# Seven half-size products for gate and value in the last two blocks of an attention and GEGLU kernel, over a fixed turn of PSUM banks

## The chip, the cores and the metric

The kernel runs on one core of one Trainium2 chip. The metric is the device time of one execution in microseconds (us). Each batch of runs was taken on one chip together with fresh runs of the kernel before; its medians were 344.80, 344.44 and 344.56 us in the three batches.

Engines in the profile: PE is TensorE, DVE is VectorE, ACT is ScalarE, POOL is GpSimd. In a timeline the columns are start (us), duration (us), engine, source line, operation, output<-inputs, shapes, count, and in brackets the idle time before it with its releaser. Matmul ends are modelled, so starts are what counts. The same statement has other line numbers in each kernel (the multiply that makes hid is L325 before and L340 after).

## The reference, cut to what matters

```python
# attention without softmax, 8 batches x 8 heads x 576 tokens x 64
kv  = einsum('bhsd,bhse->bhde', k, v)
out = einsum('bhsd,bhde->bhse', q, kv)
x   = out / rms(out) * g_norm                  # 4608 tokens x 512 after a transpose
# GEGLU and a gated residual
hid = gelu(x @ w_gate) * (x @ w_val)           # 512 -> 1536, twice
y   = x + sigmoid(x @ w_res) * (hid @ w_out)   # 1536 -> 512
```

The tokens are cut into nine blocks of 512. Block 8 holds what is left of the eight batches (64 tokens of each); a batch's part of it is called the remainder. While TensorE multiplies block b, the other engines prepare the attention of the next batch.

## The kernel before: the parts that matter

Gate and value of a block are twelve slots, each with four matmuls of 512 columns for gate and four for value. Each slot takes two PSUM banks (the buffers that matmuls write to, eight in all) from a rotating pool of four. The bank of gate comes free when ScalarE has made Gelu of it, the bank of value when VectorE has made `hid`. In the traces `t` is the attention output after its norm, `osb` the output tile, and `ws` and `ts` are the change's sums of weights and of tokens.

```python
pmoe  = ctx.enter_context(tc.tile_pool(name="pmoe",  bufs=4, space=bass.MemoryType.PSUM))
pattn = ctx.enter_context(tc.tile_pool(name="pattn", bufs=4, space=bass.MemoryType.PSUM))

def m_gval(blk, f, pool=pmoe, tag="mm"):
    ...
    gps = pool.tile([P, NJ * P], FP32, tag=tag, name="gps")
    m_mm(gps, wg_c, f, blk, 0, NJ)
    vps = pool.tile([P, NJ * P], FP32, tag=tag, name="vps")
    m_mm(vps, wv_c, f, blk, 0, NJ)
    m_act(blk, f, gps, vps)        # ge = Gelu(gps) on ScalarE, hid = ge * vps on VectorE

def m_res(blk, j, pool=pmoe, tag="mm"):
    rps = pool.tile([P, C], FP32, tag=tag, name="rps")
    ...                            # four matmuls of 512 columns, then Tanh on ScalarE
```

Behind the slots come four residual tiles (`m_res`), then the output product, which is already made of seven products of half size (Strassen's scheme in Winograd's form):

```python
def res(jj):
    for j in (2 * jj, 2 * jj + 1):
        m_res(blk, j)
    if jj == 1:
        pmoe.tile([P, C], FP32, tag="mm", name="none")   # keeps the turn even
...
prod(w["E"], a_of(blk, 1, 2), b_of(2, 1), False)
pf((0, 0), w["E"])                                 # VectorE
prod(w["A"], s_[2], wo_t[:, 2], False)
sub(nc.vector, c22, w["A"], w["d"], ALU.add)       # frees w["A"] for the last product
prod(w["F"], s_[3], b_of(2, 2), False)
...
prod(w["A"], a_of(blk, 2, 2), wo_t[:, 3], False)   # the last product
```

## Time and profile before

| | kernel before |
|---|---|
| time, median of three runs | 344.58 us (344.43 to 345.43) |
| span of the profiled run | 345.4 us |
| TensorE busy | 331.9 us, 96% |
| VectorE busy | 236.5 us, 68% |
| GpSimd busy | 103.1 us, 30% |

The span is the time between the first and the last record on the core. The device time is about 2 us longer than the span of the same run.

The waits of TensorE, costliest first (in us: total, how often, longest), show that it waits for nearly nothing behind the opening:

```profile
PE kvp L718 <- DVE v L689: 2.5, 2, 2.3
PE wA L431 <- DVE wF L404: 1.2, 1, 1.2
PE idle L668 <- DVE zeros L641: 1.2, 1, 1.2
PE vps L783 <- DVE t L757: 0.6, 1, 0.6
PE vps L336 <- DVE hid L325: 0.4, 1, 0.4
```

Only the second of these (in block 1, at 91.35 us) and the last (in block 2, at 117.72) lie outside the opening.

### The profile page before, as it was taken

The page shows a single profiled execution, that of the slowest core. Times are in us where ns is not written, and L with a number is a line of the kernel's source. Part 1 is how long each engine was busy: PE and PEld are TensorE (multiplying, and loading weights), DVE is VectorE, ACT ScalarE, POOL GpSimd, SP SyncE. Part 2 cuts the span into 40 slices and gives each one's busy share as a digit, 9 for nine tenths or more (in the row PEclk, how much of TensorE's full clock was granted, in tenths as well). Part 3 has the DMA queues.
Part 4 walks back from the last instruction along what each step waited for, and adds up shares of the span by engine and source line. Part 5 has one row for each costly group of instructions (what it writes and reads, how often), then busy time and mean ns, then how long its engine had stood idle before and what let it go on. Part 6 is the DMA issues. An engine that isn't in the chain of part 4 may idle for free.

```text
span 345.4 us, 6165 instructions
## 1 busy us (share of the span) xinstructions
PE 331.9 (96%) x2432; PEld 188.0 (54%) x2432; DVE 236.5 (68%) x446; ACT 150.1 (43%) x265; POOL 103.1 (30%) x121
## 2 busy tenths in 40 slices
PE   8789999999899999999999999999999999999992
PEld 3544454445744475447544764476447644764481
DVE  5665549769859987698578976885688735453643
ACT  3573384274336352535263615361736133623350
POOL 2692161980064108200820083005000600050013
PEclk9899999999999999999999999999999999999997
DMA  7999999669589263966395439744003120030004
GB/s 244 290 178 204 195 204 166 168 95 150 117 108 164 94 123 120 165 60 128 130 167 43 102 114 174 79 92 153 17 0 61 63 76 2 1 121 4 0 2 121
DMA packets 76399, 38.81 MB, mean 112 GB/s; under 512 B 42066, under 2 KB 73810, under 8 KB 76370
## 3 DMA queue, kind: packets, MB, share of 16 engines
q0 software_dynamic: 38752, 17.17, 40.1%
q1 hardware_dynamic: 37184, 20.71, 21.6%
q10 hardware_dynamic: 434, 0.52, 0.5%
q8 instruction: 19, 0.31, 0.4%
q14 instruction: 10, 0.08, 0.1%
HBM read 38.80 MB, written 9.44 MB: 140 GB/s over the span
## 4 chain that ended last, share of the span: by engine, by line
PE 69%; DVE 2%; issue 0%; POOL 0%; POOLq 0%; DVEq 0%
PE gps L336 21%; PE vps L336 20%; PE wA L431 10%; PE rps L356 6%; PE wF L431 3%; PE wD L431 2%; PE w L431 2%; PE wE L431 2%; PE kvp L187 1%; PE op L205 1%; DVE t L282 1%; DVE hid L325 1%; DVE hid_s L404 0%; DVE t L296 0%; POOL osb L526 0%
## 5 line engine op out<-in xcount | busy, mean ns | idle before, releaser
L324 ACT ACTIVATE ge<-gps 128x512 f16<-128x512 f32 x108 | 64.3, 597 | 133.1 <-PE gps L336 127.8
L325 DVE TENSOR_TENSOR hid<-ge,vps 128x512 f16<-128x512 f16 x108 | 73.8, 684 | 63.2 <-PE vps L336 60.8
L336 PE MATMUL vps<-xT,wv 128*128 128x512 f16 x424 | 108.8, 379 | 0.4 <-DVE hid L325 0.4
L336 PE MATMUL gps<-xT,wg 128*128 128x512 f16 x424 | 109.0, 379 | 0.0
L470 POOL TENSOR_TENSOR osb<-osb,t 128x512 f32<-128x512 f32 x28 | 36.1, 1309 | 155.6 <-DVE osb L466 148.6
L336 PEld LDWEIGHTS <-wv 128*128 128x128 f16 x424 | 41.5, 98 | 50.6 <-issue 0.7
L336 PEld LDWEIGHTS <-wg 128*128 128x128 f16 x424 | 40.2, 98 | 45.4 <-issue 0.4
L431 PEld LDWEIGHTS <-hid_s 128*128 128x128 f16 x384 | 37.5, 98 | 6.3 <-issue 1.4
L356 PE MATMUL rps<-wr,xT 128*128 128x512 f16 x144 | 32.7, 379 | 0.0
L431 PEld LDWEIGHTS <-hid 128*128 128x128 f16 x288 | 28.2, 98 | 5.1
L365 ACT ACTIVATE th<-rps 128x512 f32<-128x512 f32 x36 | 21.5, 597 | 19.0 <-PE rps L356 19.0
L356 PEld LDWEIGHTS <-xT 128*128 128x128 f16 x144 | 14.1, 98 | 16.8
L224 DVE TENSOR_REDUCE ss<-sq 128x8 f32<-128x512 f32 x32 | 20.6, 679 | 2.9 <-ACT sq L222 2.7
L431 PE MATMUL wA<-wo_ts,hid_s 128*128 128x256 f16 x168 | 20.6, 273 | 1.2 <-DVE wF L404 1.2
L370 ACT ACTIVATE th<-th 128x512 f32<-128x512 f32 x36 | 19.9, 622 | 0.0
L282 DVE TENSOR_TENSOR t<-op,ny 128x512 f16<-128x512 f32 x28 | 17.9, 682 | 0.1
L222 ACT ACTIVATE sq<-op 128x512 f32<-128x512 f32 x28 | 15.3, 597 | 4.5 <-PE op L205 4.2
L296 DVE TENSOR_TENSOR t<-t,g 128x512 f16<-128x512 f16 x36 | 16.2, 498 | 0.1
L404 DVE TENSOR_TENSOR hid_s<-hid 128x1536 f16<-128x1536 f16 x16 | 15.3, 955 | 0.3
L526 POOL TENSOR_TENSOR osb<-osb,t 128x512 f32<-128x512 f32 (+1 forms) x4 | 4.3, 1078 | 27.8 <-DVE osb L522 27.8
L373 PE MATMUL fps<-wo,hid 128*128 128x512 f16 x48 | 11.2, 379 | 0.0
L431 PE MATMUL wD<-wo_ts,hid_s 128*128 128x256 f16 x84 | 10.3, 273 | 0.1
(133 smaller groups left out, 326.5 us busy)
## 6 DMA issues: line engine op xcount, KB each, us to landing
out_dram<-osb SPq DMA_DIRECT2D x14, 512.0 KB, 2.6
qraw<-in_q_dram POOLq DMA_DIRECT2D x7, 512.0 KB, 8.2
kraw<-in_k_dram POOLq DMA_DIRECT2D x7, 512.0 KB, 9.9
v<-in_v_dram POOLq DMA_DIRECT2D x7, 512.0 KB, 11.9
out_dram<-osb SPq DMA_DIRECT2D x5, 256.0 KB, 2.8
wg<-in_moe_w_gate_dram POOLq DMA_DIRECT2D x2, 512.0 KB, 9.2
wv<-in_moe_w_val_dram POOLq DMA_DIRECT2D x2, 512.0 KB, 9.4
wo<-in_moe_w_out_dram POOLq DMA_DIRECT2D x2, 512.0 KB, 14.2
```

The costliest lines, as they stand in the source:

```text
L222: nc.scalar.activation(out=sq, in_=src, func=AF.Square)
L224: nc.vector.tensor_reduce(out=out_, in_=sq, op=ALU.add, axis=mybir.AxisListType.X)
L282: nc.vector.tensor_tensor(out=t, in0=o, in1=scale, op=ALU.mult)
L296: nc.vector.tensor_tensor(out=t_t[blk][:, jj, :], in0=t_t[blk][:, jj, :], in1=g16, op=ALU.mult)
L324: nc.scalar.activation(out=ge, in_=gps, func=AF.Gelu)
L325: nc.vector.tensor_tensor(out=hids[blk][:, f, :], in0=ge, in1=vps, op=ALU.mult)
L336: nc.tensor.matmul(ps[:, j0 * P : j1 * P], lhsT=w[:, cc, :], rhs=xT_t[blk][:, j0:j1, cc, :], start=(cc == 0 and j0 == 0), stop=(cc == NP - ...
L356: nc.tensor.matmul(rps, lhsT=xT_t[blk][:, j, cc, :], rhs=wr16[:, cc, :], start=(cc == 0), stop=(cc == NP - 1),)
L365: nc.scalar.activation(out=th, in_=rps, func=AF.Tanh, scale=0.5)
L370: nc.scalar.activation(out=th, in_=th, func=AF.Copy, scale=0.5, bias=0.5)
L431: nc.tensor.matmul(ps[:, e - es[0], :], lhsT=a[:, f, e * P : (e + 1) * P], rhs=b[:, f, :], start=(start and e == es[0] and f == 0), stop=( ...
L470: nc.gpsimd.tensor_tensor(out=res_all[of], in0=res_all[of], in1=t_t[blk][of], op=ALU.add)
```

## The change

It takes matmul time from TensorE. In blocks 7 and 8, gate and value are computed in three groups of seven half-size products instead of eight. For that, sums of quarters of the weights and of the tokens must be made by VectorE and GpSimd. The weight sums are made in block 6, in buffers that attention no longer needs. The groups use all eight PSUM banks, so the two rotating pools become one pool with a fixed tag a bank, and a small class gives out the banks in a fixed turn, in every block.

```diff
-    pmoe = ctx.enter_context(tc.tile_pool(name="pmoe", bufs=4, space=bass.MemoryType.PSUM))
-    pattn = ctx.enter_context(tc.tile_pool(name="pattn", bufs=4, space=bass.MemoryType.PSUM))
+    psum = ctx.enter_context(tc.tile_pool(name="psum", bufs=1, space=bass.MemoryType.PSUM))
+    class Banks:
+        ...
+        def tile(self, shape, dtype, name, tag=None, bank=None):
+            if bank is None:
+                n = self.n - len(self.opening)
+                bank = self.turn[n % 4] if n >= 0 else self.opening[n]
+                self.n += 1
+            self.last = bank
+            return psum.tile(shape, dtype, tag=f"bank{bank}", name=name)
+    pmoe, pattn = Banks((3, 2, 1, 0), (0, 1, 2)), Banks((4, 5, 6, 7))
 ...
-    moep = ctx.enter_context(tc.tile_pool(name="moep", bufs=3))
+    moep = ctx.enter_context(tc.tile_pool(name="moep", bufs=5))
 ...                                      # the sums of tokens of block 7, inside block 6's output products
             pf((0, 0), w["E"])
+            for f in rest:
+                f()
             prod(w["A"], s_[2], wo_t[:, 2], False)
 ...                                      # a group: digits are products, E a copy, d a copy, F and c sums, g Gelu, h hidden values
+        for word in """1g 1v Eg 5g Ev 5v dg 6g dv 6v Fg 2g Fv 2v 7g g11 7v cg 3g cv 3v h11 g22 4g g12 h12 * 4v g21 h22 h21""".split():
 ...                                      # banks of block 6's residuals, and the sums
+    out_at = {LAST[0] - 1: {j: 4 + j for j in range(NJ)}}
+            if blk == LAST[0]:
+                for j, f in enumerate(token_sums(B, nc.gpsimd, "kraw")):
+                    plan.setdefault(j * 2, []).append(f)
+            if blk == LAST[0] - 1:
+                units = [(n, g) for g in range(NF // GF) for n in "gv"]
+                todo = [f for u in units[:4] for f in weight_sums(u, nc.gpsimd)]
+                for j, f in enumerate(todo):
+                    plan.setdefault(2 + j // 2, []).append(f)
+                todo = [f for u in units[4:] for f in weight_sums(u, nc.vector)]
+                for j, f in enumerate(todo):
+                    plan.setdefault(3 + j // 2, []).append(f)
+                rest = token_sums(LAST[0], nc.vector, "qraw")
```

More of the change, by code (lines that the diff above doesn't have):

```diff
@@ L55, with __init__ @@
     hidp = ctx.enter_context(tc.tile_pool(name="hidp", bufs=1))
-    moep = ctx.enter_context(tc.tile_pool(name="moep", bufs=3))
+    moep = ctx.enter_context(tc.tile_pool(name="moep", bufs=5))
     finp = ctx.enter_context(tc.tile_pool(name="finp", bufs=2))
-    pmoe = ctx.enter_context(tc.tile_pool(name="pmoe", bufs=4, space=bass.MemoryType.PSUM))
-    pattn = ctx.enter_context(tc.tile_pool(name="pattn", bufs=4, space=bass.MemoryType.PSUM))
+    psum = ctx.enter_context(tc.tile_pool(name="psum", bufs=1, space=bass.MemoryType.PSUM))
+    class Banks:
+        def __init__(self, turn, opening=()):
+            self.turn, self.opening, self.n, self.last = turn, opening, 0, None
+        def tile(self, shape, dtype, name, tag=None, bank=None):
[6 more added lines that the diff above has]
+    pmoe, pattn = Banks((3, 2, 1, 0), (0, 1, 2)), Banks((4, 5, 6, 7))
     ctx.enter_context(tc.manual_schedule())
@@ L351, in m_gval, with m_res @@
         m_act(blk, f, gps, vps)
-    def m_res(blk, j, pool=pmoe, tag="mm"):
-        rps = pool.tile([P, C], FP32, tag=tag, name="rps")
+    def m_res(blk, j, bank=None):
+        rps = pmoe.tile([P, C], FP32, name="rps", bank=bank)
         for cc in range(NP):
@@ L438, in prod, with out_by_products @@
                 )
-    def out_by_products(blk, later):
+    out_banks = {}
+    def out_by_products(blk, later, banks=None, rest=()):
         w = {}
         s_ = hid_sums
+        banks = banks or {}
         def res(jj):
             for j in (2 * jj, 2 * jj + 1):
-                m_res(blk, j)
-            if jj == 1:
-                pmoe.tile([P, C], FP32, tag="mm", name="none")
+                m_res(blk, j, banks.get(j))
+            if jj == 1 and 3 not in banks:
+                pmoe.n += 1
         def first_two():
             for n in ("D", "E", "F", "A"):
-                w[n] = pmoe.tile([P, 2, CH], FP32, tag="mm", name="w" + n)
+                w[n] = pmoe.tile([P, 2, CH], FP32, name="w" + n, bank=banks.get(n))
+                out_banks[n] = pmoe.last
             w["d"] = finp.tile([P, 2, CH], FP32, tag="wd", bufs=1, name="wd")
@@ L508, in out_by_products, with out_last, bank @@
         return [lambda: res(0), lambda: res(1), first_two, others]
-    def out_last(blk):
+    def out_last(blk, banks):
         s_ = hid_sums
-        def bank(n, pool, tag):
-            return pool.tile([P, n, CH], FP32, tag=tag, name="w")
+        def bank(n, i):
+            return pmoe.tile([P, n, CH], FP32, name="w", bank=i)
         def part(j, n, ch):
@@ L533, in run @@
         def run():
-            wa = [bank(1, pattn, "at") for _ in range(2)]
-            wd, we, wf = [bank(2, pmoe, "mm") for _ in range(3)]
+            wa = [bank(1, banks["A"][e]) for e in range(2)]
+            wd, we, wf = [bank(2, banks[n]) for n in "DEF"]
             d = finp.tile([P, 2, CH], FP32, tag="wd", bufs=1, name="wd")
@@ L549, in run @@
             plus(0, 2, 0, nc.gpsimd)
-            m_res(blk, 3)
+            m_res(blk, 3, banks[3])
             m_sigmoid(3)
@@ L567, in run, with pairs_of @@
             store(2, 2, 0, CH)
-        return [lambda: [m_res(blk, j) for j in range(3)], run]
+        return [lambda: [m_res(blk, j, banks[j]) for j in range(3)], run]
+    LAST = (B - 1, B)
+    GF = 4
+    gv_sums, x_sums = {}, {}
+    def pairs_of(ws, f0):
+        i, o = 0, f0 * P
+        while o >= WCS[i]:
+            i, o = i + 1, o - WCS[i]
+        n = min(WCS[i] - o, GF * P)
+        parts = [ws[i][:, :, o : o + n]]
+        if n < GF * P:
+            parts.append(ws[i + 1][:, :, 0 : GF * P - n])
+        return [p.rearrange("p c (r i f) -> p r i c f", i=2, f=P) for p in parts]
@@ new lines, in w_quadrant, with weight_sums, one @@
+    def w_quadrant(ws, f0, i, k):
+        return [p[:, :, i, 2 * k : 2 * k + 2, :] for p in pairs_of(ws, f0)]
+    def weight_sums(unit, eng):
+        n, g = unit
+        ws = wg_c if n == "g" else wv_c
+        def one(s_, x, y, op):
+            if s_ == 0:
+                tag = ("q16", "k16", "v16")[len(gv_sums) // 2]
+                gv_sums[unit] = qkvp.tile([P, 4, 2, 2, P], FP16, tag=tag, name="ws")
+            sums = gv_sums[unit]
+            of = {t: w_quadrant(ws, GF * g, *t) for t in (x, y) if not isinstance(t, int)}
+            parts = len(w_quadrant(ws, GF * g, 0, 0))
+            for e in range(parts):
+                rs = slice(e * 2 // parts, (e + 1) * 2 // parts)
+                x_, y_ = (sums[:, t, rs] if isinstance(t, int) else of[t][e] for t in (x, y))
+                sub(eng, sums[:, s_, rs], x_, y_, op)
+        return [
+            lambda: one(0, (1, 0), (1, 1), ALU.add),
+            lambda: one(1, 0, (0, 0), ALU.subtract),
+            lambda: one(2, (0, 0), (1, 0), ALU.subtract),
+            lambda: one(3, (0, 1), 1, ALU.subtract),
+        ]
@@ new lines, in x_quadrant, with token_sums, one @@
+    def x_quadrant(blk, k, j):
+        return xT_t[blk][:, 2 * j : 2 * j + 2, 2 * k : 2 * k + 2, :]
+    def token_sums(blk, eng, tag):
+        def one(i, x, y):
+            if i == 0:
+                x_sums[blk] = stage.tile([P, 4, 2, 2, P], FP16, tag=tag, name="ts")
+            t = x_sums[blk]
+            x_, y_ = (t[:, n] if isinstance(n, int) else x_quadrant(blk, *n) for n in (x, y))
+            sub(eng, t[:, i], x_, y_)
+        return [
+            lambda: one(0, (0, 1), (0, 0)),
+            lambda: one(1, (1, 1), 0),
+            lambda: one(2, (1, 1), (0, 1)),
+            lambda: one(3, (1, 0), 1),
+        ]
@@ new lines, in gv_group, with tile_of, product, seed @@
+    def gv_group(blk, g, banks, amid=()):
+        if g == 0:
+            hids[blk] = hidp.tile([P, NF, NJ * P], FP16, tag="hid", name="hid")
+        f0 = GF * g
+        ps, ge, sb = {}, {}, {}
+        def tile_of(n, u):
+            ps[n, u] = pmoe.tile([P, 2, PR], FP32, name=n + u, bank=banks[u, n])
+            return ps[n, u]
+        def product(p, u):
+            ws = wg_c if u == "g" else wv_c
+            n = {1: "A", 2: "E", 3: "F", 4: "A", 5: "F", 6: "A", 7: "A"}[p]
+            first = p in (1, 5)
+            out_ = tile_of(n, u) if first else ps[n, u]
+            s_of = {3: 3, 5: 0, 6: 1, 7: 2}
+            t_of = {4: 3, 5: 0, 6: 1, 7: 2}
+            quad = {1: (0, 0), 2: (0, 1), 4: (1, 1)}
+            xq = {1: (0, 0), 2: (1, 0), 3: (1, 1)}
+            for r in range(2):
+                for c in range(2):
+                    if p in s_of:
+                        lhsT = gv_sums[u, g][:, s_of[p], r, c, :]
+                    else:
+                        i, k = quad[p]
+                        parts = w_quadrant(ws, f0, i, k)
+                        lhsT = parts[0][:, r, c, :] if len(parts) == 1 else parts[r][:, 0, c, :]
+                    rhs = x_sums[blk][:, t_of[p], :, c, :] if p in t_of else x_quadrant(blk, *xq[p])[:, :, c, :]
+                    nc.tensor.matmul(
+                        out_[:, r, :],
+                        lhsT=lhsT,
+                        rhs=rhs,
+                        start=(first and r == 0 and c == 0),
+                        stop=(c == 1),
+                        skip_group_check=True,
+                    )
+        def seed(u):
+            nc.scalar.copy(out=tile_of("E", u), in_=ps["A", u])
+        def keep(u):
+            sb["d", u] = attnp.tile([P, 2, PR], FP32, tag="sq", name="d")
+            nc.scalar.copy(out=sb["d", u], in_=ps["F", u])
+        def plus(u, n):
+            if n == "F":
+                dst = tile_of("F", u)
+            else:
+                dst = sb["c", u] = attnp.tile([P, 2, PR], FP32, tag="o32", name="c")
+            nc.vector.tensor_tensor(out=dst, in0=ps["A", u], in1=sb["d", u], op=ALU.add)
+        quarter = {"11": ("E", 0, 0), "12": ("F", 0, 1), "21": ("A", 1, 0), "22": ("c", 1, 1)}
+        def source(q, u):
+            n = quarter[q][0]
+            return sb[n, u] if n == "c" else ps[n, u]
+        def gelu(q):
+            ge[q] = moep.tile([P, 2, PR], FP16, tag="ge", name="ge")
+            nc.scalar.activation(out=ge[q], in_=source(q, "g"), func=AF.Gelu)
+        def hidden(q):
+            _, i, j = quarter[q]
+            dst = hids[blk][:, f0 + i : f0 + GF : 2, j * PR : (j + 1) * PR]
+            eng = nc.gpsimd if q == "22" else nc.vector
+            eng.tensor_tensor(out=dst, in0=ge[q], in1=source(q, "v"), op=ALU.mult)
+        for word in """1g 1v Eg 5g Ev 5v dg 6g dv 6v Fg 2g Fv 2v 7g g11 7v cg 3g cv 3v h11 g22 4g g12 h12 * 4v g21 h22 h21""".split():
+            if word == "*":
+                for f in amid:
+                    f()
+            elif word[0].isdigit():
+                product(int(word[0]), word[1])
+            elif word[0] == "E":
+                seed(word[1])
+            elif word[0] == "d":
+                keep(word[1])
+            elif word[0] in "Fc":
+                plus(word[1], word[0])
+            elif word[0] == "g":
+                gelu(word[1:])
+            else:
+                hidden(word[1:])
@@ L932, in plan_attn, with banks_of @@
             at(m, NF + 3, lambda: a_x(b, NJ), lambda: d_xT(b, NJ, NJ + 1))
+    out_at = {LAST[0] - 1: {j: 4 + j for j in range(NJ)}}
+    def banks_of(blk):
+        if blk == LAST[0]:
+            w = out_banks
+            first = {"g": (w["D"], w["F"], w["E"], w["A"]), "v": (4, 5, 6, 7)}
+        else:
+            w = out_at[LAST[0]]
+            first = {"g": (w[0], w[2], w["D"], w["A"]), "v": (w[1], w[3], w["E"], w["F"])}
+        groups = []
+        for g in range(NF // GF):
+            groups.append({})
+            for u, (a0, e, f, a1) in first.items():
+                if g % 2:
+                    a0, e, f = a1, f, e
+                groups[g].update({(u, "A"): a0, (u, "E"): e, (u, "F"): f})
+        (ga0, ge_, gf, ga1), (va0, ve, vf, va1) = first["g"], first["v"]
+        out_at[blk] = {0: ga1, 1: va1, 2: ge_, 3: ve}
+        if blk == LAST[0]:
+            out_at[blk].update(A=gf, D=vf, E=ga0, F=va0)
+        else:
+            out_at[blk].update(A=(gf, vf), D=ga0, E=va0, F=ga1)
+        return groups
     late = []
@@ L947 @@
             slots = [lambda f=f: m_gval(blk, f) for f in range(NF)]
+            sevens = blk in LAST
+            if sevens:
+                slots = [None] * NF
+                ends = banks_of(blk)
+                mid = [lambda: s_begin(blk)]
+                for g in range(NF // GF):
+                    slots[GF * g] = lambda g=g: gv_group(blk, g, ends[g], mid if g == 2 else ())
             if blk == 1:
@@ L952, with products @@
             slots += [lambda i=i: outs[i]() for i in range(4 if blk < B else 2)]
-            plan.setdefault(NFH + 2, []).insert(0, lambda: s_begin(blk))
-            def products(blk=blk, outs=outs):
+            if not sevens:
+                plan.setdefault(NFH + 2, []).insert(0, lambda: s_begin(blk))
+            if blk == LAST[0]:
+                for j, f in enumerate(token_sums(B, nc.gpsimd, "kraw")):
+                    plan.setdefault(j * 2, []).append(f)
+            rest = ()
+            if blk == LAST[0] - 1:
[7 more added lines that the diff above has]
+                rest = token_sums(LAST[0], nc.vector, "qraw")
+            def products(blk=blk, outs=outs, rest=rest):
                 s_rest(blk)
-                outs.extend(out_by_products(blk, blk == 1) if blk < B else out_last(blk))
+                outs.extend(
+                    out_by_products(blk, blk == 1, out_at.get(blk), rest) if blk < B else out_last(blk, out_at[blk])
+                )
             plan.setdefault(NF - 1, []).append(products)
```

## The prediction

> **What bounds the kernel now.** I read four views in this order: the page, the timeline of TensorE in blocks 6 to 8, the timelines of VectorE and GpSimd over the same stretch, and the waits of TensorE.
>
> The page first:
>
> ```profile
> PE 331.9 (96%) x2432; PEld 188.0 (54%) x2432; DVE 236.5 (68%) x446; ACT 150.1 (43%) x265; POOL 103.1 (30%) x121
> PE   8789999999899999999999999999999999999992
> PE gps L336 21%; PE vps L336 20%; PE wA L431 10%; PE rps L356 6%; PE wF L431 3%; PE wD L431 2%; PE w L431 2%; PE wE L431 2%; PE kvp L187 1%; PE op L205 1%; DVE t L282 1%; DVE hid L325 1%; DVE hid_s L404 0%; DVE t L296 0%; POOL osb L526 0%
> ```
>
> TensorE is busy in 96% of the span, in nines in nearly every slice, and the chain that ended last is TensorE work. In such a kernel matmul time that is taken away shortens the run one for one, and any new wait of TensorE lengthens it one for one. The timeline of TensorE in block 7 shows how tight it is:
>
> ```profile
> 271.75 1.03 PE L336 MATMUL gps<-xT,wg 128*128 128x512 f16 x4
> 272.62 1.03 PE L336 MATMUL vps<-xT,wv 128*128 128x512 f16 x4
> ...
> 292.47 3.62 PE L356 MATMUL rps<-wr,xT 128*128 128x512 f16 x16
> 295.93 1.47 PE L431 MATMUL wA<-wo,hid 128*128 128x256 f16 x12
> 297.24 1.47 PE L431 MATMUL wD<-wo_ts,hid_s 128*128 128x256 f16 x12
> ```
>
> Columns: start, duration with its modelled end, instruction. Starts are what counts. Gate and value of block 7 run from 271.75 to 292.47, 20.72 us for 96 matmuls of 512 columns, so 215.9 ns each. Twelve matmuls of 256 columns take 297.24 - 295.93 = 1.31 us, so 109.2 ns each. Nothing idles between.
>
> VectorE is the second engine to watch, in block 6 above all:
>
> ```profile
> 250.77 0.69 DVE L325 TENSOR_TENSOR hid<-ge,vps 128x512 f16<-128x512 f16 x1 [0.39 <-PE vps L336]
> 252.50 0.69 DVE L325 TENSOR_TENSOR hid<-ge,vps 128x512 f16<-128x512 f16 x1 [1.04 <-PE vps L336]
> ...
> 260.58 1.42 DVE L296 TENSOR_TENSOR t<-t,g 128x512 f16<-128x512 f16 x4
> ...
> 262.63 0.96 DVE L404 TENSOR_TENSOR hid_s<-hid 128x1536 f16<-128x1536 f16 x1
> ```
>
> After the idle 1.04 us at 252.50 VectorE has no idle time until 265. Its first sum of hidden values (262.63, done 263.6) serves the product wD at 263.89: only 0.3 us of slack at the end of block 6. Blocks 7 and 8, which have no attention beside them, leave VectorE idle 1.04 us of every 1.73.
>
> Last, what VectorE and GpSimd do to each other, from their timelines at 61 and at 273 us:
>
> ```profile
> 61.26 1.66 DVE L107 COPY q<-qraw 128x2048 f16<-128x2048 f16 x1
> 62.33 5.38 POOL L404 TENSOR_TENSOR wo_ts<-wo,wo_ts 128x512 f16<-128x512 f16 x4
> 63.44 1.04 DVE L107 COPY k<-kraw 128x2048 f16<-128x2048 f16 x1
> ...
> 271.41 4.40 POOL L470 TENSOR_TENSOR osb<-osb,t 128x512 f32<-128x512 f32 x3 [1.29 <-DVE osb L466]
> 273.54 1.26 DVE L296 TENSOR_TENSOR t<-t,g 128x512 f16<-128x512 f16 x1
> ```
>
> The multiply t<-t,g takes 0.42 us alone (four in 1.42 us at 260.58, so 0.34 apart) but 1.26 us at 273.54, beside GpSimd. The four wo_ts operations at 62.33 take 5.38 us, where GpSimd needs 1.13 us each undisturbed (three in 3.38 us at 66.56).
>
> **What the Trainium skill says.** (1) "TensorE: Matmul & The Clock Gate", section "Back-to-back issue gap": 262 cycles for 256 columns, 109.2 ns at 2.4 GHz. The trace agrees (109.2 ns). (2) "SBUF — State Buffer", section "SBUF: two separate sides": the port pair that VectorE and GpSimd share is an exclusive lock; a GpSimd operation, or a VectorE operation with two SBUF inputs or in a two-port mode, holds it for the whole instruction and the other blocks. The trace agrees: 0.42 becomes 1.26 us, while hid (one of its inputs in PSUM) stays at 0.67 to 0.69 us beside GpSimd. (3) "GPSIMD Engine Reference", section "Elementwise — side-by-side cycle accounting": about 2.6 cycles an element with two inputs. At 1.2 GHz that is 1.11 us for 512 elements, as in the trace, so I estimate 0.62 us for 256 (half, and some overhead); no row shows that form without a VectorE conflict.
>
> **The change, part by part.**
>
> Removed: 96 matmuls of 512 columns in each of blocks 7 and 8, 20.72 us a block. Added: 3 groups x 7 products x 2 (gate, value) x 4 matmuls of 256 columns = 168, at 109.2 ns 18.35 us. Gain 2.38 us a block, 4.76 us in all, if TensorE never waits. That is 1.4% of 344.6, so even a perfect change does not reach 2%.
>
> Waits inside a group. A group is 14 slots of 0.437 us, 6.12 us. ScalarE has 4 copies and 4 Gelus, 4.7 us at 0.57 to 0.60; VectorE 4 sums and 3 products, at most 4.8 us at 0.69 (0.60 apart). Both fit. Following the order: the sum Fg can start 2.46 us into the group (after product 6 and ScalarE's copy d) and ends at 3.15; product 7 of gate, which needs it, has its slot at 3.50. Fv ends at 3.75, its slot is at 3.93; the sums c end at 4.90 and 5.50, their slots are at 5.24 and 5.68. Slack is 0.1 to 0.3 us everywhere, so I count no wait in the steady state. At the end of a block the third group's last hid ends some 2.1 us after the group, the first sum at 3.1, the second at 4.1; residual (3.45 us, 2.6 in block 8) and the first product (1.31) cover both. In the first group of block 7 VectorE is late with the remainder's t and its multiply (they end 3.05 us after the block's start in the trace before): 0.3 us.
>
> Added to block 6, VectorE: eight sums of weights (512 elements, 16 bit, two SBUF inputs; like t<-t,g, 0.42 us) in pairs in slots 3 to 6. GpSimd: 16 sums of 256 and 8 of 512, 16 x 0.62 + 8 x 1.12 = 18.9 us from 239.9 (when the last output sum of block 5 ends) to about 259, exactly where VectorE's pairs fall.
> I walked VectorE's queue by hand with the rows' durations. A value bank comes free when hid is done, and TensorE needs it two slots later.
> - Without conflict: pairs of 0.8 us. The idle time after slot 3 (1.9 us) takes most of 3.2 us; TensorE waits 0.9 us.
> - With the lock, each sum after the first waits for a GpSimd operation, and GpSimd for it: about 1.3 us a sum. Pair 1 ends at 248.3, pair 2 at 252.7, hid of slot 5 at 253.4 (249.8 before); the value matmuls of slot 7 start 253.5, not 251.36: 2.1 us. Pair 3 ends at 256.4, hid 6 at 257.1: 4.05 in all. Pair 4 ends 258.9, hid 7 at 259.6: 4.9. The norm (2.4 us and a last wait) and hid 8, 263.0: 6.5 us.
>
> Residual banks of block 6: they are now those of attention, and the order by engine shows the first residual waiting for the third t, which VectorE reaches behind hid of slot 10: 1.3 us more, in both cases.
>
> Token sums of block 7: four sums on VectorE between pf(0,0) (268.79) and the sum c22, which the last product waits for at 270.44. They take 1.6 us, so c22 ends at 271.1: 0.7 us. But GpSimd's first output sum (268.96) starts between the first and the second of them and holds the lock for 1.15 us: then 1.5 us.
>
> Sum with the lock: -4.76 + 6.5 + 1.3 + 1.5 + 0.3 = +4.8 us, 349.4. Without: -4.76 + 0.9 + 1.3 + 0.7 + 0.3 = -1.6 us, 343.0.
>
> **Rivals.**
> (a) The gain arrives whole: about 340. For it: the order is laid out so that every bank is free in time, and the third group's slack holds in my walk. Against: VectorE's end of block 6 has 0.3 us of slack and gets eight operations more.
> (b) The lock hits in full: 349 to 350. For it: the two rows above, and wo_ts and k alternating at 62 to 64 us. Against: someone placed these sums one pair a slot, presumably having seen them run; if GpSimd gets through 256 elements faster or is ahead of the pairs, half of the 6.5 us goes.
> (c) A bank or a sum inside the groups is late by more than my 0.1 us slack: each 0.1 us costs up to 2 waits x 6 groups, 1.2 us. ScalarE to TensorE latencies are little seen in the trace before, which hardly waits: up to +2 us.
>
> **Range and chances.** I give the lock 70% and the unlocked case 30%, and take the middle, a gain that is eaten: 347.5 us. The range 341.8 to 351.0 holds the unlocked case and most of the locked one. Faster by over 2% (below 337.7) is beyond the 4.76 us that there is: 3%, for a mistake of mine. Slower by over 2% (above 351.5) needs the lock and 2 us more: 12%. Within 2%: 85%.
>
> **What would show it.** Right: 18.3 to 18.7 us for gate and value of blocks 7 and 8; TensorE waits of some us on hid in slots 7 to 10 of block 6, VectorE's sums of weights at 1.2 to 1.4 us each, GpSimd busy some 19 us there; a wait of the first residual of block 6 on t; a wait of wA on osb before block 7. Wrong: sums of weights at 0.42 us beside GpSimd (the lock step falls); block 6 as long as before (35.25 us; the queue walk falls); groups longer than 6.3 us (the slack inside a group falls). A run at 340 would say that block 6 absorbs everything.

## More of the kernel before

In the printed run the clock dipped in the opening (the second digit of this row, the granted clock in tenths over 40 slices):

```profile
PEclk9899999999999999999999999999999999999997
```

So the page's 345.4 us is a slow example: the 21 later runs of this kernel had spans of 342.4 to 344.0 us.

## The result, and the profile after

| | before | after |
|---|---|---|
| time, median of four runs | 344.50 us (344.36 to 345.43) | 356.96 us (355.60 to 357.15) |
| span, profiled run | 345.4 us | 353.8 us |
| TensorE busy, profiled run | 331.9 us | 329.1 us |

The ratio is 1.0349, with a 95% interval of 1.0328 to 1.037: slower. (A ratio here is the mean time of one kernel's fast runs over that of the other's fast runs of the same rounds, so it is not quite the ratio of the medians.) The prediction, 347.5 us with a range up to 351.0, was wrong by 9.5 us. The outputs are right.

The page's lines that answer to those shown of the kernel before (busy time of the engines, TensorE in tenths over 40 slices, the chain by line):

```profile
PE 329.1 (93%) x2576; PEld 200.9 (57%) x2576; DVE 257.8 (73%) x476; ACT 161.2 (46%) x289; POOL 134.5 (38%) x155
PE   8889999999899899999999999999858899999992
PE gps L351 10%; PE vps L351 9%; PE wA L446 9%; PE rps L371 4%; DVE hid L340 4%; PE Av L680 3%; PE Ag L680 3%; DVE t L297 3%; PE w L446 2%; PE wD L446 2%; PE wF L446 2%; PE wE L446 2%; DVE ws L419 2%; PE Fg L680 1%; PE Fv L680 1%
```

TensorE has less to do, as intended, but four slices fall to 8, 5, 8 and 8 in block 6, and in the chain VectorE's `hid` and `t` now take 4% and 3% instead of 1% each, with 2% for the new `ws`. The waits of TensorE name the places:

```profile
PE vps L351 <- DVE hid L340: 6.8, 5, 2.4
PE rps L371 <- DVE hid L340: 3.2, 4, 1.1
PE gps L948 <- DVE t L922: 1.3, 1, 1.3
PE wA L446 <- DVE osb L419: 1.2, 1, 1.2
...
PE rps L371 <- DVE t L297: 1.1, 1, 1.1
...
PE Ag L680 <- DVE Fg L701: 0.8, 1, 0.8
```

The first, fourth, fifth and sixth are terms that the prediction has. Of the first, 0.8 us lies in block 2 and 6.0 in block 6. The second (four residual waits in blocks 2 to 5) and the third (the opening) are in blocks where the prediction counted nothing.

In block 6, VectorE's sums of weights (`ws`) stand between the multiplies that free value's banks:

```profile
253.12 0.41 DVE L419 TENSOR_TENSOR ws<-wg 128x512 f16<-128x512 f16 x1
253.45 1.37 DVE L419 TENSOR_TENSOR ws<-wg,ws 128x512 f16<-128x512 f16 x1
...
255.94 1.28 DVE L419 TENSOR_TENSOR ws<-wv 128x512 f16<-128x512 f16 x1
257.26 1.25 DVE L419 TENSOR_TENSOR ws<-ws,wv 128x512 f16<-128x512 f16 x1
258.43 0.67 DVE L340 TENSOR_TENSOR hid<-ge,vps 128x512 f16<-128x512 f16 x1
```

GpSimd makes its sums at the same time, for example:

```profile
253.16 1.38 POOL L419 TENSOR_TENSOR ws<-wg 128x512 f16<-128x512 f16 x1
254.62 1.22 POOL L419 TENSOR_TENSOR ws<-ws,wg 128x512 f16<-128x512 f16 x1
```

A sum that takes 0.41 us alone (all eight take 0.41 or 0.42 in the trace of e3_no_pool, below, where GpSimd has none) takes 1.25 to 1.37 in four of the eight cases here. The other four took 0.41, 0.73, 0.77 and 0.77. TensorE's value matmul at 259.16 waits for the `hid` at 258.43:

```profile
259.16 1.02 PE L351 MATMUL vps<-xT,wv 128*128 128x512 f16 x4 [1.80 <-DVE hid L340]
```

In block 3, VectorE's order and TensorE's residuals of the kernel before:

```profile
153.94 1.28 DVE L282 TENSOR_TENSOR t<-op,ny 128x512 f16<-128x512 f32 x2
155.14 1.42 DVE L296 TENSOR_TENSOR t<-t,g 128x512 f16<-128x512 f16 x4
156.48 0.68 DVE L325 TENSOR_TENSOR hid<-ge,vps 128x512 f16<-128x512 f16 x1
```

```profile
153.78 3.62 PE L356 MATMUL rps<-wr,xT 128*128 128x512 f16 x16
157.23 1.47 PE L431 MATMUL wA<-wo,hid 128*128 128x256 f16 x12
```

The last `hid` of the block stands behind `t` and `t<-t,g` and ends at 157.16. All sixteen residual matmuls run from 153.78 without a gap: none of their four banks needs that `hid`. After the change VectorE has the same order, shifted by 0.27 us:

```profile
155.41 1.42 DVE L311 TENSOR_TENSOR t<-t,g 128x512 f16<-128x512 f16 x4
156.75 0.68 DVE L340 TENSOR_TENSOR hid<-ge,vps 128x512 f16<-128x512 f16 x1
```

```profile
154.04 2.75 PE L371 MATMUL rps<-wr,xT 128*128 128x512 f16 x12
157.48 1.02 PE L371 MATMUL rps<-wr,xT 128*128 128x512 f16 x4 [0.68 <-DVE hid L340]
```

The fourth residual is now cut off from the other three. It waits for the last `hid`, whose bank the fixed turn gives it.

The seven products do what they should. In the trace after, gate and value of block 8 run from 316.00 to the residuals at 334.34, 18.34 us; the same stretch took 20.72 us in a trace with 512-column matmuls.

### The profile page after: what moved, and what is told of

The parts are those of the page before. It is cut to its first block, busy times and chain, and to the rows that moved or that the text cites. A ratio compares the mean times of both kernels' runs of the same rounds, so it can differ in the third digit from the quotient of the medians.

```text
span 353.8 us, 6550 instructions
## 1 busy us (share of the span) xinstructions
PE 329.1 (93%) x2576; PEld 200.9 (57%) x2576; DVE 257.8 (73%) x476; ACT 161.2 (46%) x289; POOL 134.5 (38%) x155
## 4 chain that ended last, share of the span: by engine, by line
PE 53%; DVE 16%; issue 3%; ACT 1%; POOLq 0%; POOL 0%; DVEq 0%
PE gps L351 10%; PE vps L351 9%; PE wA L446 9%; PE rps L371 4%; DVE hid L340 4%; PE Av L680 3%; PE Ag L680 3%; DVE t L297 3%; PE w L446 2%; PE wD L446 2%; PE wF L446 2%; PE wE L446 2%; DVE ws L419 2%; PE Fg L680 1%; PE Fv L680 1%
## 5 line engine op out<-in xcount | busy, mean ns | idle before, releaser
L339 ACT ACTIVATE ge<-gps 128x512 f16<-128x512 f32 x84 | 50.0, 597 | 105.1 <-PE gps L351 104.3
L351 PE MATMUL vps<-xT,wv 128*128 128x512 f16 x328 | 84.2, 379 | 6.8 <-DVE hid L340 6.8
L340 DVE TENSOR_TENSOR hid<-ge,vps 128x512 f16<-128x512 f16 x84 | 57.2, 682 | 40.3 <-PE vps L351 38.0
L351 PE MATMUL gps<-xT,wg 128*128 128x512 f16 x328 | 84.3, 380 | 0.0
L351 PEld LDWEIGHTS <-wv 128*128 128x128 f16 x328 | 32.1, 98 | 46.3 <-issue 8.2
L351 PEld LDWEIGHTS <-wg 128*128 128x128 f16 x328 | 30.8, 98 | 34.4 <-issue 0.2
L371 PE MATMUL rps<-wr,xT 128*128 128x512 f16 x144 | 33.5, 379 | 4.3 <-DVE hid L340 3.2
L680 PEld LDWEIGHTS <-ws 128*128 128x128 f16 x192 | 18.8, 98 | 3.3 <-issue 1.2
L717 POOL TENSOR_TENSOR hid<-ge,c 128x512 f16<-128x512 f16 x6 | 7.0, 1162 | 20.7 <-ACT ge L711 20.7
L446 PE MATMUL wA<-wo_ts,hid 128*128 128x256 f16 x84 | 10.3, 272 | 1.2 <-DVE osb L419 1.2
```

What stands on the lines that cost most here:

```text
L339: nc.scalar.activation(out=ge, in_=gps, func=AF.Gelu)
L340: nc.vector.tensor_tensor(out=hids[blk][:, f, :], in0=ge, in1=vps, op=ALU.mult)
L351: nc.tensor.matmul(ps[:, j0 * P : j1 * P], lhsT=w[:, cc, :], rhs=xT_t[blk][:, j0:j1, cc, :], start=(cc == 0 and j0 == 0), stop=(cc == NP - ...
L371: nc.tensor.matmul(rps, lhsT=xT_t[blk][:, j, cc, :], rhs=wr16[:, cc, :], start=(cc == 0), stop=(cc == NP - 1),)
L446: nc.tensor.matmul(ps[:, e - es[0], :], lhsT=a[:, f, e * P : (e + 1) * P], rhs=b[:, f, :], start=(start and e == es[0] and f == 0), stop=( ...
L680: nc.tensor.matmul(out_[:, r, :], lhsT=lhsT, rhs=rhs, start=(first and r == 0 and c == 0), stop=(c == 1), skip_group_check=True,)
```

## The experiments

The theory after the traces had four parts: (1) the fixed turn alone costs time in blocks that the change doesn't otherwise touch; (2) in block 6 VectorE and GpSimd block each other; (3) single operands are late at the end of block 6; (4) the products give their whole 4.76 us. The main rival to (1) was that the residual waits come from somewhere else (more buffers, a later VectorE), the rival to (2) that VectorE just has too much to do, with or without GpSimd.

### The bank turn alone (e1_banks)

```diff
-            sevens = blk in LAST
+            sevens = False
 ...                       # and no sums, no banks for the groups
```

> Only the fixed turn of PSUM banks (and the five Gelu buffers); gate and value of all blocks by eight full products as before, no sums of weights or tokens. Theory A (the fixed turn gives the fourth residual of blocks 2 to 6 the bank of the last value group, so it waits for a hid that VectorE reaches only after the t and x of attention): about +0.9 us in each of blocks 2 to 6, so 348.5 to 349.5 us, with TensorE's wait of rps on hid at 4 to 5 us in all. Rival B (the turn is neutral, and the 2.9 us that the changed kernel is late at the start of block 6 came from the opening or from chance): 344 to 345.5 us, no wait of rps on hid.

Measured: 350.61 us (350.35 to 351.35), ratio 1.0173 (1.0158 to 1.0188). The turn alone costs 5.8 us, even more than expected. Its waits of TensorE:

```profile
PE rps L371 <- DVE hid L340: 4.0, 5, 1.1
PE gps L948 <- DVE t L922: 1.3, 1, 1.3
```

There are five residual waits, blocks 2 to 6, since block 6's residuals are on the turn as well here. The 1.3 us in the opening weren't in the expectation.

### Both repairs of the turn (e9_banks)

This is the same kernel with the residuals on the order of the kernel before, and with the opening's second gate tile on the bank of the idle matmuls. The numbers in `res` are positions in the turn.

```diff
-    pmoe, pattn = Banks((3, 2, 1, 0), (0, 1, 2)), Banks((4, 5, 6, 7))
+    pmoe, pattn = Banks((3, 0, 1, 2), (0, 1, 2, 3, 0, 1, 2)), Banks((4, 5, 6, 7))
 ...
+                b = [pmoe.turn[(n + i) % 4] for i in range(4)]
+                w["res"] = (b[0], b[2], b[1], b[0])      # the fourth reuses the first one's bank
+                pmoe.turn, pmoe.opening, pmoe.n = (b[1], b[0], b[3], b[2]), (), 0
 ...
-                m_res(blk, j, banks.get(j))
+                m_res(blk, j, banks[j] if 3 in banks else w["res"][j])
```

> Only the fixed bank turn (as in the run with the turn alone, no seven products and no sums) with both repairs of it: the residuals of blocks 1 to 7 on the bank order of the kernel before, and the opening's second gate tile on the idle matmuls' bank. Theory A (the turn alone cost 5.8 us, through these two places and no third): the time returns to that of the kernel before, 344.4 us, ratio 0.999 to 1.003. Rival B (one tag a bank or five buffers of Gelu have a further cost): 345.5 to 347 us.

Measured: 344.54 us (344.18 to 345.49), ratio 0.9994 (0.9967 to 1.0021). The time is back at that of the kernel before, and both waits shown above are gone from its list. So the turn costs through these two places, and a third, the five Gelu buffers or one tag a bank cost nothing that can be seen (the interval is 1.1 us less to 0.7 us more). Why the rotating pool gave the residuals their old order isn't shown; the order itself is the one named in the expectation of e2_res.

### The changed kernel with the residuals repaired (e2_res)

The edit is the part of the last one that concerns `res`, for blocks 1 to 5.

> The changed kernel, but the four residuals of blocks 1 to 5 take the banks that they had before (last two gate banks, one value bank, then the first residual's bank again). Theory A: the waits of rps on hid in blocks 2 to 5 (3.2 us) go, 353 to 354 us. Rival B: no change, 356.5 to 357.5 us.

Measured: 352.09 us (351.76 to 353.46), ratio 1.022 (1.0197 to 1.0242), so 4.9 us less than the changed kernel. That is below the range expected. The residual waits on hid are gone. They were 3.2 us by the list, and 3.7 by the starts of the matmuls (table below); the rest goes with the granted clock, 0.992 or 0.993 in three of the four runs against 0.986 to 0.990 in three of the changed kernel's four (see e8_open). The fourth run, at a clock of 0.989, took 353.46 us, 3.5 below the changed kernel at 0.990 (356.97).

### The opening's bank (e8_open)

```diff
-    pmoe, pattn = Banks((3, 2, 1, 0), (0, 1, 2)), Banks((4, 5, 6, 7))
+    pmoe, pattn = Banks((3, 0, 1, 2), (0, 1, 2, 3, 0, 1, 2)), Banks((4, 5, 6, 7))
```

> The changed kernel with only the order of the four first banks in the opening changed: the second gate tile takes the bank of the idle matmuls instead of the bank of the second attention output. Theory A (the fixed turn costs 1.2 us in the opening, by the wait of 1.28 us of the second gate tile on the last multiply t): that wait goes, another of 0.6 us of a value tile on t may come as in the kernel before, and the time falls by 0.6 to 1.3 us against the changed kernel (356.97), to about 356. Rival B (the opening is bound by the loads, the wait only shows them): less than 0.3 us.

Measured: 355.87 us (355.59 to 356.03), ratio 1.0325 (1.0309 to 1.034): 1.1 us less, as theory A has it. The 1.3 us wait went, and a wait of `vps` on `t` of 0.6 us came, as in the kernel before.

This trace also showed something that the changed kernel's own doesn't. VectorE's first sum of weights:

```profile
248.01 4.37 DVE L419 TENSOR_TENSOR ws<-wg 128x512 f16<-128x512 f16 x1
```

It is the same 512-element sum, and it took 4.37 us (as it did in e2_res's trace). It got through only when GpSimd's run of 256-element sums was over and its first 512-element sum had ended. TensorE then waited 3.51 us at a stretch, and after that its clock was down, to 0.57 in the second row (each row: stretch, length, busy us of PE, PEld, DVE, ACT, POOL, then granted clock, DMA share, GB/s):

```profile
254.32 1.87 PE L351 MATMUL vps<-xT,wv 128*128 128x512 f16 x4 [3.51 <-DVE hid L340]
255.97 1.85 PE L351 MATMUL gps<-xT,wg 128*128 128x512 f16 x4
```

```profile
248.00:254.00 6.00, 2.81 (x14) 1.18 (x12) 5.97 (x4) 1.57 (x3) 5.92 (x8) 1.00 0.00 0
254.00:258.00 4.00, 3.51 (x8) 1.17 (x8) 4.00 (x7) 1.25 (x3) 3.92 (x4) 0.57 0.00 0
258.00:262.00 4.00, 2.18 (x10) 0.95 (x10) 3.97 (x6) 1.06 (x2) 2.78 (x3) 1.00 0.00 0
```

Four matmuls of 512 columns start 1.65 us apart here (254.32 to 255.97) instead of 0.86. The Trainium skill's page "TensorE: Matmul & The Clock Gate", section "HAM oscillation — how this bites in real kernels", says that TensorE must not idle longer than some 3.4 us. Of six traces with GpSimd's packed sums in block 6, those with a single wait of 3.51 (this one), 3.52 (e2_res) and 4.29 us (e4_no_dve, below) show the half clock behind it, one with 3.50 us (e5_swap, below) doesn't, and the changed kernel's own and that of e6_tok, with nothing above 2.4 us, don't either. That fits the page, though the 3.50 us show that the limit isn't sharp here. It also makes the changed kernel's runs easier to read: the one that was profiled took 355.60 us at a clock of 0.996, the other three 356.95 to 357.15 at 0.986 to 0.990. Their traces weren't kept, so that they had this long wait is inferred, not seen.

### GpSimd's sums taken away (e3_no_pool), VectorE's taken away (e4_no_dve)

Both give wrong results: the products use the sums that are left.

```diff
 # e3_no_pool
-                todo = [f for u in units[:4] for f in weight_sums(u, nc.gpsimd)]
-                for j, f in enumerate(todo):
-                    plan.setdefault(2 + j // 2, []).append(f)
 # e4_no_dve
-                todo = [f for u in units[4:] for f in weight_sums(u, nc.vector)]
-                for j, f in enumerate(todo):
-                    plan.setdefault(3 + j // 2, []).append(f)
```

> The changed kernel without GpSimd's 24 sums of weights in block 6 (their users read the sums of the third group instead, so the result is wrong on purpose); VectorE keeps its eight. Theory L (the shared port: VectorE's two-input operations wait for GpSimd's): VectorE's sums take 0.42 us instead of 1.0 on average, the waits of vps on hid in block 6 fall from 6.0 to about 1 us, the run to 351 to 352.5 us. Rival Q (the eight more operations in VectorE's queue are what costs, the port little): waits stay at 4 us or more, 355 us or more.

Measured: 349.73 us (349.45 to 349.83), ratio 1.0143 (1.0128 to 1.0158).

```profile
PE vps L351 <- DVE hid L340: 1.3, 2, 0.8
```

VectorE has all its eight sums still, and yet of 6.8 us of waits on `hid` 1.3 are left, 0.8 of them a wait that this list also has where there are no sums at all (e9_banks). So it isn't VectorE's load: by the starts of the matmuls its eight sums alone cost 0.7 us in block 6. The time is below the range expected. The gain of 7.2 us holds the lower clock of the median; against the changed kernel's run at the same clock (355.60 at 0.996) it is 5.9 us, and the waits on `hid` fell by 5.5.

> The changed kernel without VectorE's eight sums of weights (their users read GpSimd's, wrong on purpose); GpSimd keeps its 24 operations in block 6. Theory L: GpSimd is still at work when VectorE reaches the norm of attention (12 small operations, most with two SBUF inputs), which then crawls: a wait of 4 to 5 us of vps on hid in one place, run 354.5 to 356 us. Rival Q: with the eight gone no wait over 1 us is left, 350.5 to 352 us.

Measured: 354.02 us (353.61 to 354.67), ratio 1.027 (1.0252 to 1.0289).

```profile
PE vps L351 <- DVE hid L340: 5.1, 2, 4.3
```

Without VectorE's sums 4.3 of the 6.0 us of waits in block 6 are still there, in one piece: VectorE's norm (small operations) crawls beside GpSimd, and the clock was 0.987 or 0.988. Two operations of the norm, beside GpSimd:

```profile
256.79 1.20 DVE L273 TENSOR_SCALAR nh<-nm 128x40 f32<-128x40 f32 x1
258.13 1.11 DVE L276 TENSOR_TENSOR na<-na,nh 128x40 f32<-128x40 f32 x1
```

In the kernel before they took 0.18 and 0.20 us. The first has a single input, so one input alone doesn't keep a VectorE operation from being stretched. The time is 0.5 us below the range expected. So VectorE's sums are cheap without GpSimd's, but GpSimd's aren't without VectorE's, since they also hit what VectorE has to do anyway.

### All weight sums on GpSimd, over four blocks (e7_spread)

```diff
+                    3: lambda: weight_sums(("g", 0), nc.gpsimd),
+                    4: lambda: weight_sums(("v", 0), nc.gpsimd),
+                    5: lambda: weight_sums(("g", 1), nc.gpsimd) + half[:2],
+                    6: lambda: half[2:] + weight_sums(("g", 2), nc.gpsimd) + weight_sums(("v", 2), nc.gpsimd),
 ...                       # the first group's sums get two tiles of their own
```

> The changed kernel with all 48 weight-sum operations' work on GpSimd and none on VectorE, spread over blocks 3 to 6 (the first group's sums in tiles of their own in blocks 3 and 4, the rest in blocks 5 and 6) instead of being packed into block 6. Theory A (the lock between VectorE and GpSimd in block 6 delays VectorE's hid, and that and the clock it lowers cost some 6.6 to 8 us): the waits of the value matmuls of block 6 on hid (6.0 us in the changed kernel's trace) fall below 1.5 us, the granted clock is 0.993 or more, and the time is 348 to 350.5 us. Rival B (GpSimd costs VectorE the same wherever its sums stand, since TensorE has no slack in blocks 3 to 5 either): waits on hid appear in blocks 3 to 5 and the time stays above 353 us.

Measured: 348.36 us (348.22 to 348.65), ratio 1.0109 (1.0094 to 1.0124), clock 0.994 to 0.998: 8.6 us less than the changed kernel's median, and 7.2 less than its run at a like clock (355.60). Theory A holds and B falls.

```profile
PE rps L372 <- DVE hid L341: 3.2, 4, 1.1
PE gps L953 <- DVE t L927: 1.3, 1, 1.3
...
PE vps L352 <- DVE hid L341: 0.8, 1, 0.8
```

The waits of block 6 on `hid` are gone; the residual waits and the opening's stay. GpSimd is busier in all than in the changed kernel (142.4 us against 134.5), and has still ten sums in block 6, one of which I show with what VectorE does at the same time:

```profile
250.58 1.16 POOL L420 TENSOR_TENSOR ws<-ws,wv 128x512 f16<-128x512 f16 x1
```

```profile
250.57 1.27 DVE L240 TENSOR_REDUCE ss<-sq 128x8 f32<-128x512 f32 x2
251.76 0.68 DVE L341 TENSOR_TENSOR hid<-ge,vps 128x512 f16<-128x512 f16 x1
```

Neither is stretched. `hid` has one input in PSUM, and the reduction has one input. GpSimd's last sum of block 6 ended at 253.97, and the norm, which e4_no_dve shows to crawl beside such sums, began at 255.75; in blocks 3 to 5 the sums end before the norm too. Which VectorE operation stands beside GpSimd decides, not how much GpSimd has to do.

### Block 7's token sums on GpSimd (e6_tok)

```diff
-                rest = token_sums(LAST[0], nc.vector, "qraw")
+                tokens = token_sums(LAST[0], nc.gpsimd, "qraw")
+                for f in tokens:
+                    plan.setdefault(NF + 1, []).append(f)
```

> The changed kernel with block 7's four token sums on GpSimd at the end of block 6's values, instead of on VectorE among the output products of block 6. Theory A (on VectorE they delay the sum c22 that the last output product waits for): the wait of wA on osb of 1.2 us goes and the time falls by about 1.2 us, to 355.7. Rival B (they block each other through the lock there too, and the multiplies of the residuals come later): no gain, or the wait turns up at the first residual or at the first product that needs the token sums in block 7.

Measured: 354.03 us (353.04 to 355.12), ratio 1.0273 (1.0239 to 1.0307). The four runs fall in two pairs: 353.04 twice at a clock of 0.994 and 0.997, and 355.02 and 355.12 at 0.985. Against the changed kernel at like clocks that is 2.6 and 1.9 us, more than I expected. The reason is in the list: the wait of `wA` on `osb` (1.2 us) is gone, and with it that of `Ag` on `Fg` in the first group of block 7 (0.8 us), since VectorE reaches that sum earlier.

### The banks of block 6's residuals swapped (e5_swap)

```diff
-    out_at = {LAST[0] - 1: {j: 4 + j for j in range(NJ)}}
+    out_at = {LAST[0] - 1: dict(enumerate((6, 7, 4, 5)))}
```

> The changed kernel with the four residuals of block 6 on attention banks 6, 7, 4, 5 in turn instead of 4, 5, 6, 7, so that the first one takes a bank whose multiply t comes earlier. Theory A (my predicted term of 1.3 us for the bank of t stands by itself): the wait of the first residual on t (1.1 us) goes and the time falls by about 1.1 us against the changed kernel's 356.97, to 355.9, if the clock is the same. Rival B (VectorE's queue is what TensorE waits for there, whatever the bank): the wait comes back at the next residual or at the first output product, and the time stays within 0.4 us.

Measured: 355.16 us (354.23 to 356.30), ratio 1.0299 (1.0262 to 1.0336). The wait of the first residual on `t` is gone, and 0.2 us of it comes back as a wait of `wA` on `hid`. Of the runs, two at a clock of 0.996 took 354.23 and 354.29, so 1.3 us less than the changed kernel at the same clock; the profiled one took 356.02, because its first sum of weights took 4.35 us and TensorE waited 3.50 us for what stood behind it. Theory A holds in the trace; the median alone, with two patterns mixed in four runs, wouldn't carry it.

### All repairs (best3), and one more (best4)

The five edits above in one kernel:

> All repairs at once on the changed kernel: old bank order for the residuals of blocks 1 to 5, weight sums on GpSimd over blocks 3 to 6, the banks of block 6's residuals swapped, block 7's token sums on GpSimd, and the opening's banks reordered. If the separate terms are right and add up (356.97 less 4.9 for the residuals, 7 for the spread sums with the clock, 1.2 for the swap, 1.3 for the token sums, 1.0 for the opening) the time is 341 to 342.5 us, so faster than the kernel before by the 2.4 us a block that were promised less what is left: ratio 0.989 to 0.994. If they overlap (one wait only uncovers the next), 344 to 347 us.

Measured: 341.08 us (340.88 to 342.19), ratio 0.9907 (0.9883 to 0.993). The terms add up: the gain is 15.9 us, and the five of the expectation make 15.4. (The five measured alone, each against the median of 356.96, would make 19.3; several of them hold the median's lower clock.) What it still waits for behind the opening:

```profile
PE wA L447 <- DVE wF L420: 1.2, 1, 1.2
...
PE vps L352 <- DVE hid L341: 0.8, 1, 0.8
PE Ag L688 <- DVE Fg L709: 0.8, 1, 0.8
```

The first two are in blocks 1 and 2, and also in e9_banks. The third is the last remainder's norm on VectorE, stretched by GpSimd's output sums. Moved behind the first group of block 7:

```diff
-            at(m, NF + 3, lambda: a_t(b, NJ))
+            end = (m, NF + 3) if m < B - 2 else (m + 1, 0)
+            at(*end, lambda: a_t(b, NJ))
```

> The repaired kernel of 341.08 us with one thing more: the last remainder's multiply t and its norm on VectorE, and the transposition behind them, moved from the end of block 6 to behind the first group of block 7. The wait of Ag on Fg in the first group (0.77 us) comes from VectorE reaching Fg late behind that norm, which takes 1.27 us beside GpSimd's output sums. If so, 340.2 to 340.5 us. If the transposition then comes too late for GpSimd's token sums of block 8, hidden values on GpSimd are late in group 2 and the time is 341 us or more.

Measured: 340.81 us (340.54 to 341.83), ratio 0.9879 (0.9851 to 0.9906). The wait of `Ag` is gone, but one of `Av` on `c` of 0.4 us took its place, and the gain over best3, 0.3 us, is within the spread of both, and just short of what I expected. Compared by the starts of the same instructions, the profiled run of best4 was 1.9 us behind that of e9_banks before block 7 (1.7 of it lost to the loads of the opening) and 2.4 us ahead at the end. So blocks 7 and 8 gave 4.2 us: the products' 4.76 less 0.6 at that wait (`Ag` at 275.94, `Av` at 276.96, 1.02 us apart instead of 0.44).

## Why the prediction was wrong

To size the terms I compared the starts of the same TensorE instructions in the changed kernel's trace and in that of e9_banks (span 342.4 us, the kernel before in all that matters, without the dip of the clock in the opening of its printed page). Where the difference of the starts steps, a term lies:

| term | predicted | measured step |
|---|---|---|
| the loads of the opening (differ from run to run) | 0 | +0.8 |
| second gate tile of the opening on the bank of `t` | not seen | +1.3 |
| fourth residual of blocks 2, 3, 4, 5 | not seen | +1.2, 0.8, 0.9, 0.8 |
| VectorE's queue in block 6, waits on `hid` | +6.5 (70%) or +0.9 | +6.6 |
| first residual of block 6 on `t` | +1.3 | +1.3 |
| token sums of block 7, last product waits | +1.5 or +0.7 | +1.4 |
| first group of block 7 | +0.3 | +1.1 |
| products, two blocks | -4.76 | -4.76 |
| sum | +4.8 or -1.6 | +11.4 |

(Block 7's step is -1.24 us in all; its products are put at the -2.38 measured in block 8, and the rest is given to its first group.)

**The step that failed** is "The change, part by part". It counts the products, the sums and the banks of block 6, and has no line for the change of the pools to a fixed turn, which touches every block. That is 5.0 us in the table and 5.8 us by itself (e1_banks, where block 6 pays too), and e9_banks shows that it is those two places. I had the order of the instructions by engine and read it for block 6 only, where it did show the wait on `t`. The same reading for the fourth residual of any other block would have shown that its bank is the one of the last value tile, and VectorE's timeline says when that comes free.

**What was right.** The wait on `t` (1.3), the token sums (1.5 and 1.4) and the places of the four waits in block 6 (slots 7 to 10) came out as they were worked out. With GpSimd's sums away, VectorE's eight cost 0.7 us (e3_no_pool), near the 0.9 of the unlocked case. The gain of the products is exact in block 8, where gate and value took 18.34 us of the 18.3 to 18.7 that I gave; block 7 took 19.48, of which the first group's 1.1 is the excess. The slack inside a group held behind that first group, where no wait of the groups is in the list; in the first group a sum was late, so rival (c) falls only for the rest. Rival (b) is nearest to what happened in block 6, and rival (a) fell.

**What was right in part by luck.** The locked sum's walk of block 6 gave 6.5 us and 6.6 were measured, but not by the same parts. The walk's four waits add up to 2.1, 4.05, 4.9 and 6.5 us; measured were 1.2, 3.2, 4.1 and 6.6. Four of the eight sums took 0.41 to 0.77 us where the walk has about 1.3 for all but the first, so VectorE was 0.8 us ahead of it after the third wait. From there to the end of the next `hid` the walk has 3.4 us (the norm, 2.4, a last wait and the `hid`). It took 4.3, since the norm took 3.7 (261.62 to 265.28) beside GpSimd, which was done only at 263.2, and that made up for it.

**What was mis-sized.** The first group cost 1.1 us, not 0.3: besides the remainder's norm, the token sums on VectorE delayed it (e6_tok took the 0.8 us wait away and left 0.4). And the weighing took the middle: with the lock in full the prediction's own sum was 349.4, and it put 30% on the unlocked case because "someone placed these sums one pair a slot, presumably having seen them run". The rows at 62 us and 273 us that it cites were evidence; that was not. With the lock certain, the turn's 5.0 us, the first group's 0.8 us and the 1.4 us between the changed kernel's profiled run and its median (put down to the lower clock, see e8_open) bring 349.4 to 356.6; measured were 356.96. (Its 215.9 ns a matmul should read 215.8, 20.72 us by 96, which changes nothing else.)

**What stays open.** Why VectorE's first sum gets through after 0.7 us in some traces and after 4.4 in others, with the same instructions in the same order.

## What to carry to other kernels

When a rotating pool becomes a fixed assignment, the change is in every place that takes a buffer: for each one, name the reader that frees it, and look up when that reader runs. Before moving elementwise work to a second engine, look at which operations it will stand beside, and spread it over stretches where the other engine runs operations that a trace shows unstretched (here `hid` and the reductions, not the norm); the same work that cost 6.6 us packed into one block, a third of it on VectorE, cost no wait on GpSimd over four blocks. In a kernel whose first engine is 96% busy, undo the parts of a change one by one before giving it up: here the idea was worth 1.2%, and what came with it cost 4.7% (356.96 less 340.81, over 344.50).

## What the Trainium skill lacked or had wrong

- "SBUF — State Buffer", section "SBUF: two separate sides": it says that the engine which starts first holds the shared ports for the whole instruction and the other blocks. The runs agree with that (0.41 us alone, up to 1.37 beside GpSimd, in the changed kernel's trace), but the page doesn't say that the one blocked may lose several turns in a row: a sum of 0.41 us took 4.35 us (e5_swap) and 4.37 us (e2_res and e8_open) beside GpSimd's sums, of some 0.6 us each there (pairs of them start 1.25 us apart), where in the changed kernel's own trace the same one took 0.73 us.
- "TensorE: Matmul & The Clock Gate", section "HAM oscillation — how this bites in real kernels": confirmed by waits of 3.51, 3.52 and 4.29 us with a half clock behind them, and by waits of up to 2.38 us without. A wait of 3.50 us had none, so a wait near the limit may or may not cost it.
- The same page, section "Back-to-back issue gap", gives about 131 ns a matmul for 512 columns in a sustained stream with weight loads, and calls its formula's 216 ns too high there. Here such a stream takes 215.8 ns a matmul (96 in 20.72 us), so the formula holds and the sustained figure doesn't.
- No page that I found speaks of what a fixed order of PSUM banks costs against a rotating pool: 5.8 us of 344.8 here, by a bank given to a tile whose reader stands late in VectorE's queue.
